# Turning the experts' rows in 32 by 32 blocks on VectorE, and loading them as 96 columns a partition group

## The chip, the cores and the metric

The kernel runs on one core of a Trainium2 chip. The engines are TensorE (PE), VectorE (DVE), ScalarE (ACT), GpSimd (POOL) and SyncE (SP, which here only issues DMAs). The metric is the device time of one execution in microseconds. The median of 3 runs of the kernel before is 709.5 us.

## The reference

A gated linear attention is followed by a mixture of experts; every token goes to two of eight experts.

```python
for t in range(S):                       # attention, 4 x 8 heads, 768 steps, 48 wide
    new_re = ar * S_re - ai * S_im
    new_im = ar * S_im + ai * S_re
    kv = np.einsum('bhd,bhe->bhde', k[:, :, t], v[:, :, t])
    S_re, S_im = (new_re + kv, new_im)
    y[:, :, t] = np.einsum('bhd,bhde->bhe', q[:, :, t], S_re)
...
# x: 3072 tokens of 384 floats, E = 8 experts, F = 1024
noisy_logits = x @ w_gate + np.log1p(np.exp(x @ w_noise)) * noise
top2 = np.argpartition(-noisy_logits, 2, axis=1)[:, :2]
...
for e in range(E):
    for k in range(2):
        mask = top2[:, k] == e
        h = np.maximum(x[mask] @ w1[e], 0.0)
        out[mask] += top2_w[mask, k, None] * (h @ w2[e])
```

## The kernel before

**The stage that the change leaves alone.** Up to about 280 us the kernel computes the attention in 24 tiles, finds each token's two experts and scatters its row (L497) into `xs` in DRAM: 400 floats, of which 0 to 383 are x, 384 to 391 the gates and 392 (`RNO`) the token's number, into the next free slot of the expert. Its order is written out by hand. Part of the work of experts 0 and 1 already lies in it.

**One expert.** An expert has 832 slots in two windows. Window 1 has 512 rows and lives in `xgb`, window 0 has 320 rows and lives in `xga`. `load_x` brings a window into SBUF with several whole rows on a partition (four of 1600 bytes side by side for window 1). The matmuls want x with its 384 columns on partitions, so `x_T` turns it: for each of the three blocks of 128 columns (kk = 0, 1, 2) PE multiplies tiles of 128 by 128 with an identity into PSUM (`px`, L625; 4 for window 1, 3 for window 0), ACT rounds the result to the high half of x (L630), DVE subtracts to get the low half (L631). It also copies the gates (`gw`, L615) and the token numbers (`ox`, L616) out of the rows.

`mm1` (L633 to L656) computes relu(x w1) in eight groups (f) of 9 matmuls, 3 for each kk: high by high, low by high, high by low. ACT does the relu (L651), DVE the low half (L655, tile `h`). `mm2_tile` (L691 on) computes one output tile of 128 rows: 24 matmuls into `po` (L698), an eviction by DVE that multiplies by the gate and adds to `ao` (L709), and a scatter by POOL into `out` (L710). Before that `gather_o` has fetched the old rows of `out` into `ao` (L674). Tiles 0, 1 and 2 belong to window 0, tiles 3 to 6 to window 1; tile 2 has 64 rows (L704, L707, L708). The weights come in pieces into `raw` (3 buffers) and are split by ACT (L586) and DVE (L587) into a high and a low half; `w1` is held twice (`e % 2`), `w2` once.

**What sets the order.** Outside the attention a scheduler arranges the instructions of each engine by their dependencies and the buffers; each engine then takes its queue strictly in order. `po` has 2 buffers, `ph` 4, `px` 2, `raw` 3; there is one `xgb` and one `xga`, so that the load of the next rows waits for the last reader of the present ones. `behind_of(a, name)` puts an instruction behind the latest of a kind on the same engine: `h` is the last relu on DVE, `m` the last matmul of mm1, `po` the last matmul of mm2.

**The order of the experts.** After mm2(0, 0) the program does mm1(1, 0), x_T(0, 1), mm1(0, 1), mm2(0, 1), x_T(1, 1), mm1(1, 1), mm2(1, 1), x_T(2, 1), mm2(1, 0), x_T(2, 0), where the pair is expert and window. Then comes a loop over experts 2 to 7, the tails of which the prediction speaks: mm1 of window 1; a conditional part `mm1_tail` (L658), which does mm1 of window 0 with 320 or with 256 rows and, in the first case, tile 2 too; then the tiles 3, 4, 5, 6, 0, 1, and after each of them one block of x_T of the next expert, in the order (1,0), (1,1), (1,2), (0,0), (0,1), (0,2) of window and kk. These transposes stand on PE behind the last matmul of the tile just done.

## Time and profile before

| | us |
|---|---|
| median of 3 runs | 709.5 |
| lowest and highest | 709.18, 710.33 |
| the profiled execution, its own time | 710.01 |
| its span, first to last instruction | 708.3 |
| lies outside the span | 1.7 |

The busy times of the engines are shares of the span and add up to more than one, since the engines run side by side. PE's matmuls are pipelined: a record lasts longer than the distance to the next one, so that distances of starts tell the pace. Idle time of an engine is put down to what ended it, in square brackets in a timeline; the chain of waits follows the end of the program back to its start.

### The profile page before, as it was taken

Reading aid. Unit: us, or ns where it says so; the run is one execution under the profiler, and the core shown is the slowest. Engines: PE = TensorE matmul, PEld = TensorE weight load, DVE = VectorE, ACT = ScalarE, POOL = GpSimd, SP = SyncE. Lnnn points to the kernel's source line nnn. Section 1 sums busy time; section 2 is a strip of 40 time slices with the busy share of each in tenths; the row PEclk is TensorE's granted clock in tenths of the full one; section 3 lists DMA queues with packets and bytes.
Section 4 is the critical chain, followed back from the end, with each engine's and each line's share of the span. In section 5 each row is a group of like instructions: output and inputs, shape, how many; then the busy total and the mean of one; then the engine's idle time right before and its main releaser. Section 6 shows DMA issues by size and latency. Waiting matters only on the chain.

```text
span 708.3 us, 13293 instructions
## 1 busy us (share of the span) xinstructions
PE 666.2 (94%) x5120; PEld 590.7 (83%) x5120; DVE 411.2 (58%) x919; ACT 328.0 (46%) x553; POOL 172.6 (24%) x183
## 2 busy tenths in 40 slices
PE   2599999999998999999999999999999999999995
PEld 0388887887776889898998998998999899899995
DVE  6799899999988747545237325425524524524311
ACT  7699888888775542324125215215313413413300
POOL 3000012451404225113224122322321411411311
PEclk9989999999999999999999999999999999999998
DMA  8877863654238516325128125425415515502201
GB/s 315 255 217 211 268 181 127 174 200 131 94 92 277 178 72 249 130 84 187 59 80 264 30 91 169 129 90 169 132 40 175 179 37 178 173 23 68 65 33 36
DMA packets 64190, 100.24 MB, mean 142 GB/s; under 512 B 26296, under 2 KB 46533, under 8 KB 64112
## 3 DMA queue, kind: packets, MB, share of 16 engines
q1 hardware_dynamic: 54752, 71.68, 32.7%
q0 software_dynamic: 9360, 27.54, 11.0%
q8 instruction: 46, 0.75, 0.4%
q14 instruction: 32, 0.26, 0.1%
HBM read 68.55 MB, written 31.69 MB: 142 GB/s over the span
## 4 chain that ended last, share of the span: by engine, by line
PE 80%; DVE 8%; ACT 5%; DMA 4%; issue 1%; SPq 1%; another core or an unknown queue 0%; POOL 0%; POOLq 0%; DVEq 0%; ACTq 0%
PE po L698 28%; PE ph L649 27%; PE ptr L354 4%; PE psc L363 4%; PE pY L412 2%; PE cum L307 2%; DMA raw<-in_moe_w_dram 2%; PE pY L414 2%; PE px L625 2%; PE pG L374 2%; PE po L704 2%; PE cum L331 1%; PE psc L649 1%; ACT t L248 1%; PE cum L427 1%
## 5 line engine op out<-in xcount | busy, mean ns | idle before, releaser
L698 PE MATMUL po<-w2h,h 128*128 128x384 f32 x768 | 203.9, 338 | 2.1 <-DVE ao L709 2.1
L649 PE MATMUL ph<-x,w1h 128*128 128x512 f32 (+2 forms) x720 | 187.2, 348 | 0.6 <-ACT x L630 0.5
L698 PEld LDWEIGHTS po<-w2h,h 128*128 128x128 f32 x768 | 139.4, 188 | 3.7 <-DVE ao L709 3.6
L649 PEld LDWEIGHTS ph<-x,w1h 128*128 128x128 f32 x720 | 125.7, 189 | 18.3 <-DVE h L655 1.3
L698 PE MATMUL po<-w2l,h 128*128 128x384 f32 x384 | 128.5, 335 | 0.0
L649 PE MATMUL ph<-x,w1l 128*128 128x512 f32 (+2 forms) x360 | 124.4, 347 | 0.0
L710 POOL DMA_INDIRECT out_dram<-ao,ox x52 | 50.9, 978 | 261.2 <-DVE ao L709 247.2
L497 POOL DMA_INDIRECT xs<-xr,sl x48 | 60.8, 1266 | 202.4 <-DVE qk L336 92.0
L655 DVE SCALAR_TENSOR_TENSOR h<-ph,h 128x512 fp32r<-128x512 f32 (+2 forms) x144 | 69.6, 505 | 67.5 <-ACT h L651 51.0
L651 ACT ACTIVATE h<-ph 128x512 fp32r<-128x512 f32 (+2 forms) x120 | 59.9, 507 | 102.0 <-PE ph L649 73.3
L709 DVE SCALAR_TENSOR_TENSOR ao<-po,gw,ao 128x384 f32<-128x384 f32 (+1 forms) x52 | 31.8, 614 | 125.1 <-PE po L698 124.8
L630 ACT CAST x<-px 128x512 fp32r<-128x512 f32 (+1 forms) x42 | 21.3, 518 | 125.5 <-PE px L625 125.5
L649 PEld LDWEIGHTS ph<-x,w1l 128*128 128x128 f32 x360 | 67.9, 189 | 7.9
L698 PEld LDWEIGHTS po<-w2l,h 128*128 128x128 f32 x384 | 72.2, 188 | 0.1
L674 POOL DMA_INDIRECT ao<-out_dram,ox x49 | 54.7, 1117 | 53.7 <-issue 31.7
L363 PE MATMUL psc<-qT,kT 112*128 112x128 f32 x384 | 54.1, 283 | 1.1 <-DVE h L655 0.6
L363 PEld LDWEIGHTS psc<-qT,kT 112*128 112x128 f32 x384 | 48.9, 196 | 5.9 <-issue 1.9
L586 ACT CAST w2h<-raw 128x768 fp32r<-128x768 f32 x32 | 26.5, 835 | 33.6 <-PE po L698 17.3
L414 PE MATMUL pY<-am,v 128*48 128x128 f32 x384 | 38.3, 275 | 1.6 <-DVE am L364 1.6
L587 DVE TENSOR_TENSOR w2l<-raw,w2h 128x768 fp32r<-128x768 f32 x32 | 30.4, 957 | 15.1 <-ACT w2h L586 14.2
L364 DVE TENSOR_TENSOR am<-psc,mask 128x512 f32<-128x512 f32 x48 | 32.8, 684 | 10.2 <-PE psc L363 8.6
L412 PE MATMUL pY<-qT,z 112*48 112x128 f32 x320 | 34.2, 279 | 0.2 <-DVE z L397 0.2
(211 smaller groups left out, 936.6 us busy)
## 6 DMA issues: line engine op xcount, KB each, us to landing
raw<-in_moe_w_dram SPq DMA_DIRECT2D x24, 512.0 KB
raw<-in_moe_w_dram SPq DMA_DIRECT2D x32, 384.0 KB
qk<-in_qk_dram SPq DMA_DIRECT2D x24, 384.0 KB
xgb<-xs SPq DMA_DIRECT2D x8, 800.0 KB
v<-in_v_dram SPq DMA_DIRECT2D x24, 192.0 KB
out_dram<-zero SPq DMA_DIRECT2D x12, 384.0 KB
re<-in_a_dram SPq DMA_DIRECT2D x11, 384.0 KB
im<-in_a_dram SPq DMA_DIRECT2D x11, 384.0 KB
```

The source lines that it names most:

```text
L363: key(f"P5{'ab'[half]}.{n}", nc.tensor.matmul(p[:, j, :], KT[n][:, h, :], QT[n][:, h, :], start=True, stop=True))
L364: LAST['am'] = nc.vector.tensor_mul(AM[n][:, 4 * half:4 * half + 4, :], p, mask[:, None, :].to_broadcast([128, 4, 128]))
L412: x = nc.tensor.matmul(o, Z[b][:, h, :], QT[n][:, h, :], start=True, stop=False, skip_group_check=True)
L414: x = nc.tensor.matmul(o, V[n][:, h, :], AM[n][:, h, :], start=not g, stop=True, skip_group_check=True)
L497: d = nc.gpsimd.indirect_dma_start(out=xs, out_offset=bass.IndirectOffsetOnAxis(ap=sl[:, kk, b:b + 1], axis=0), in_=XR[g][:, lo + b, :], i ...
L649: LAST['m'] = nc.tensor.matmul(p[:, :c], W1[e, kk][i][:, f * 128:(f + 1) * 128], XW[w, kk][:, j, 0:c], start=(m == 0), stop=(m == len(ms) ...
L651: nc.scalar.activation(h[:, 0:c], p[:, :c], AF.Relu)
L655: LAST['h'] = nc.vector.scalar_tensor_tensor(h[:, dst:dst + b - a], p[:, a:b], 0.0, h[:, a:b].bitcast(F32), op0=OP.max, op1=OP.subtract)
L674: nc.gpsimd.indirect_dma_start(out=ao[j][0:w, :], out_offset=None, in_=out, in_offset=bass.IndirectOffsetOnAxis(ap=OX[e][0:w, j:j + 1], ax ...
L698: LAST['po'] = key(f"PO.{e}.{j}", nc.tensor.matmul(p[:, :DM], HT[w, f][i][:, o:o + 128], W2[f // 2][k2][:, f % 2, :], start=(m == 0), stop ...
L709: nc.vector.scalar_tensor_tensor(a, p[0:n, :DM], g, a, op0=OP.mult, op1=OP.add)
L710: d = nc.gpsimd.indirect_dma_start(out=out, out_offset=bass.IndirectOffsetOnAxis(ap=OX[e][0:n, j:j + 1], axis=0), in_=a, in_offset=None, b ...
```

## The change

`load_x` brings window 1 of every expert, and window 0 of experts 2 to 7, in another layout. Four DMAs each fill one group of 32 partitions: group a gets columns 96a to 96a + 95, and partition p of it the rows p, p + 32, p + 64 and so on, as runs of 96 floats. A 32 by 32 block transposed in place then has column 96a + 3i + kk on partition 32a + i, if every third column is taken, so three DVE transposes (L656) give the three blocks of 128 columns. The order of x's columns over partitions and kk is another one than before, and `load_w1` takes the rows of w1 in that same order. ACT and DVE read the turned block from an SBUF tile `xt` (2 buffers) instead of `px`.

Gates and token numbers no longer lie on the partitions of their rows. They come as a tile `ex` (2 buffers) by one or two DMAs of 16 floats a row; the evictions read the gate from it (L739), `ox` is cast from it (L639 to L643). For experts 2 to 7 window 1 now holds the slots 0 to 511 and window 0 the slots 512 to 831. Window 0 of experts 0 and 1 is loaded as before and turned by PE, with every third column. The memset of `xgb` goes; x_T(0, 1) stands behind `h` on DVE instead of behind `m` on PE, and the transposes of the loop are no longer tied to a tile.

```diff
     def load_x(e, w, dst):
-        if w == 0:
-            t = CAP - 64 if e in TAILS else 256
+        if w == 0 and e not in TAILS:
             ds = [nc.sync.dma_start(dst[:, 0:2], x3[e, 0:256].rearrange("(p j) r -> p j r", j=2)),
-                  nc.sync.dma_start(dst[0:64, 2], x3[e, t:t + 64])]
+                  nc.sync.dma_start(dst[0:64, 2], x3[e, 256:320])]
...
-            o = 256 if e in TAILS else 320
-            nc.sync.dma_start(dst, x3[e, o:o + 512].rearrange("(p j) r -> p j r", j=4))
+            n = WIN[w][1]
+            x = blocks(dst, n)
+            o = CAP - n if w == 0 or e not in TAILS else 0
+            for a in range(4):
+                nc.sync.dma_start(x[32 * a:32 * a + 32], x3[e, o:o + n, 96 * a:96 * a + 96].rearrange("(t p) r -> p t r", p=32))
+            if w == 0:
+                return
+            EX[e] = ex = mt([128, 7, 16], F32, name="ex", bufs=2)
+            m = 6 if e in TAILS else 4
+            nc.sync.dma_start(ex[:, 0:m], x3[e, o:o + 128 * m, DM:ROW].rearrange("(m p) r -> p m r", p=128))
+            if e in TAILS:
+                nc.sync.dma_start(ex[0:64, 6], x3[e, CAP - 64:CAP, DM:ROW])
+
+    def blocks(t, n):
+        return t.rearrange("p j r -> p (j r)")[:, 0:3 * n].rearrange("p (t r) -> p t r", r=96)
...
-            nc.sync.dma_start(r, w1[e, kk * 128:(kk + 1) * 128, :])
+            nc.sync.dma_start(r, w1[e].rearrange("(p k) f -> k p f", k=KD)[kk])
...
         for kk in kks:
             x = XW[w, kk] = mt([128, 2, n], F32R, name=f"x{w}{kk}")
-            p = ps_tile("px")
-            for j in js:
-                o = 128 * (j - js[0])
-                gz = nc.tensor.transpose(p[:, o:o + 128], src_t[:, j - js[0], kk * 128:(kk + 1) * 128], ident)
+            if rows:
+                p = ps_tile("px")
+                for j in js:
+                    o = 128 * (j - js[0])
+                    c = src_t[:, j - js[0], 0:DM].rearrange("p (i k) -> p k i", k=KD)[:, kk]
+                    nc.tensor.transpose(p[:, o:o + 128], c, ident)
+            else:
+                p = mt([128, 512], F32, name="xt", bufs=2)
+                gz = nc.vector.transpose(p[:, :n].rearrange("p (t i) -> p t i", i=32), blocks(src_t, n).rearrange("p t (i k) -> p k t i", k=KD)[:, kk])
                 if (e, w) == (0, 1):
-                    behind_of(gz, 'm')
-                if last:
-                    behind_of(gz, last)
+                    behind_of(gz, "h")
...
-        a, g = ao[j][0:n, :], GW[e][0:n, j:j + 1]
+        a = ao[j][0:n, :]
+        g = GW[e][0:n, j:j + 1] if e not in TAILS and j < 3 else EX[e][0:n, extra(e, j), e:e + 1]
...
-    nc.vector.memset(xgb, 0.0)
...
-                x_T(e + 1, x[0], (x[1],), "po")
+                x_T(e + 1, x[0], (x[1],))
```

How the order moves, at three places. In the names a number behind the underline tells one use of a buffer; the two digits in `x10`, `h07` or `w1l21` are window and kk, window and f, and kk and e % 2.

PE at x_T(0, 1), right after mm1(1, 0), before:

```order
L649 MATMUL ph_3875<-x02_3488,w1l21_3530 128x320
L625 MATMUL px_3891<-ident_58,xgb_3684 128x128 x4
L625 MATMUL px_3899<-ident_58,xgb_3684 128x128 x4
L649 MATMUL ph_3917<-x10_3890,w1h00_2720 128x512
L649 MATMUL ph_3930<-x10_3890,w1h00_2720 128x512
L649 MATMUL ph_3943<-x10_3890,w1h00_2720 128x512
L625 MATMUL px_3907<-ident_58,xgb_3684 128x128 x4
L649 MATMUL ph_3917<-x10_3890,w1h00_2720 128x512
L649 MATMUL ph_3917<-x10_3890,w1l00_2721 128x512
```

PE at the same place, after:

```order
L678 MATMUL ph_3879<-x02_3488,w1l21_3530 128x320
L907 MATMUL px_4194<-flg_4189,ones_f_99 1x2
L678 MATMUL ph_3913<-x10_3893,w1h00_2720 128x512 x2
L678 MATMUL ph_3913<-x10_3893,w1l00_2721 128x512
L678 MATMUL ph_3913<-x11_3898,w1h10_2726 128x512 x2
L678 MATMUL ph_3913<-x11_3898,w1l10_2727 128x512
L678 MATMUL ph_3913<-x12_3903,w1h20_2732 128x512 x2
L678 MATMUL ph_3913<-x12_3903,w1l20_2733 128x512
```

The transposes are gone, a matmul of a flag (L878 before, L907 after) has moved up, and the first matmuls of three groups that stood between the transposes have gone back to their groups.

DVE at x_T(0, 1), before:

```order
L655 SCALAR_TENSOR_TENSOR h07_3874<-ph_3875,h07_3874 128x64
L615 COPY gw_2848<-xgb_3684 128x4
L616 CAST ox_2849<-xgb_3684 128x4
L631 TENSOR_TENSOR x10_3890<-px_3891,x10_3890 128x512
L631 TENSOR_TENSOR x11_3898<-px_3899,x11_3898 128x512
L631 TENSOR_TENSOR x12_3906<-px_3907,x12_3906 128x512
```

DVE at the same place, after:

```order
L684 SCALAR_TENSOR_TENSOR h07_3878<-ph_3879,h07_3878 128x64
L656 STREAM_TRANSPOSE xt_3894<-xgb_3684 128x512
L643 CAST ox_2848<-ex_3696 128x4
L656 STREAM_TRANSPOSE xt_3899<-xgb_3684 128x512
L660 TENSOR_TENSOR x10_3893<-xt_3894,x10_3893 128x512
L660 TENSOR_TENSOR x11_3898<-xt_3899,x11_3898 128x512
L656 STREAM_TRANSPOSE xt_3904<-xgb_3684 128x512
L660 TENSOR_TENSOR x12_3903<-xt_3904,x12_3903 128x512
```

Three transposes now stand between the last relu and the last subtraction, the third of them behind two subtractions, since `xt` has two buffers.

DVE in the tail of expert 2, from the end of the conditional part (the branch) to the second eviction, before:

```order
L663 UNCONDITIONAL_BRANCH
L709 SCALAR_TENSOR_TENSOR ao3_3680<-po_5015,gw_4473,ao3_3680 128x384
L631 TENSOR_TENSOR x10_5048<-px_5049,x10_5048 128x512
L709 SCALAR_TENSOR_TENSOR ao4_3681<-po_5056,gw_4473,ao4_3681 128x384
L631 TENSOR_TENSOR x11_5085<-px_5086,x11_5085 128x512
```

DVE at the same place, after:

```order
L692 UNCONDITIONAL_BRANCH
L660 TENSOR_TENSOR x12_5104<-xt_5105,x12_5104 128x512
L604 TENSOR_TENSOR w1l11_4994<-raw_4991,w1h11_4993 128x1024
L656 STREAM_TRANSPOSE xt_5139<-xga_94 128x320
L604 TENSOR_TENSOR w1l21_5000<-raw_4997,w1h21_4999 128x1024
L656 STREAM_TRANSPOSE xt_5173<-xga_94 128x320
L739 SCALAR_TENSOR_TENSOR ao3_3680<-po_5003,ex_4351,ao3_3680 128x384
L660 TENSOR_TENSOR x00_5138<-xt_5139,x00_5138 128x320
L660 TENSOR_TENSOR x01_5172<-xt_5173,x01_5172 128x320
L656 STREAM_TRANSPOSE xt_5207<-xga_94 128x320
L660 TENSOR_TENSOR x02_5206<-xt_5207,x02_5206 128x320
L739 SCALAR_TENSOR_TENSOR ao4_3681<-po_5041,ex_4351,ao4_3681 128x384
```

The turning of expert 3's x and two of the splits of its w1 have moved ahead of the eviction of tile 3, the first two blocks of it even ahead of the conditional part.

## Rows read from the trace of the kernel before

**Rows 1.** The page, parts 1 and 4: busy us, share, instructions; the chain by engine.

```profile
PE 666.2 (94%) x5120; PEld 590.7 (83%) x5120; DVE 411.2 (58%) x919; ACT 328.0 (46%) x553; POOL 172.6 (24%) x183
...
PE 80%; DVE 8%; ACT 5%; DMA 4%; issue 1%; SPq 1%; another core or an unknown queue 0%; POOL 0%; POOLq 0%; DVEq 0%; ACTq 0%
```

**Rows 2.** Groups by line and shape: busy us, mean ns | idle before, releaser.

```profile
L709 DVE SCALAR_TENSOR_TENSOR ao<-po,gw,ao 128x384 f32<-128x384 f32 x48 | 29.4, 614 | 124.8 <-PE po L698 124.8
L587 DVE TENSOR_TENSOR w1l<-raw,w1h 128x1024 fp32r<-128x1024 f32 x24 | 28.8, 1219 | 1.3 <-issue 0.9 <-ACT w1h L586 0.2
L631 DVE TENSOR_TENSOR x<-px,x 128x512 fp32r<-128x512 f32 x24 | 16.3, 689 | 8.5 <-ACT x L630 8.5
L625 PE MATMUL px<-ident,xgb 128*128 128x128 f32 x96 | 13.9, 273 | 0.0
L631 DVE TENSOR_TENSOR x<-px,x 128x320 fp32r<-128x320 f32 x18 | 8.8, 486 | 1.7 <-ACT x L630 1.7
L187 DVE MEMSET pY<- 128x512 f32 x1 | 0.5, 485 | 0.1
```

**Rows 3.** The chain in order of time: start us, us, what, instructions.

```profile
291.49 16.13 PE ph L649 x69
...
327.14 15.81 PE ph L649 x68
...
413.01 4.17 PE po L698 x24
417.62 4.17 PE po L698 x24
422.12 4.17 PE po L698 x24
```

**Rows 4.** PE's timeline after tile 3 of experts 2 and 7: start us, us.

```profile
407.26 0.60 PE L625 MATMUL px<-ident,xgb 128*128 128x128 f32 x4
408.14 0.45 PE L698 MATMUL po<-w2h,h 128*128 128x384 f32 x1 [0.27 <-DVE ao L709]
...
677.84 0.34 PE L698 MATMUL po<-w2h,h 128*128 128x384 f32 x1
678.88 0.44 PE L698 MATMUL po<-w2h,h 128*128 128x384 f32 x1 [0.71 <-DVE ao L709]
```

**Rows 5.** PE's timeline where x of experts 0, 1 and 2 is turned.

```profile
288.81 1.03 PE L625 MATMUL px<-ident,xgb 128*128 128x128 f32 x8
...
324.11 1.03 PE L625 MATMUL px<-ident,xgb 128*128 128x128 f32 x8
...
359.45 1.03 PE L625 MATMUL px<-ident,xgb 128*128 128x128 f32 x8
360.24 0.42 PE L698 MATMUL po<-w2h,h 128*128 128x384 f32 x1
...
372.01 0.82 PE L625 MATMUL px<-ident,xga 128*128 128x128 f32 x6
372.58 0.71 PE L649 MATMUL ph<-x,w1h 128*128 128x512 f32 x2
```

**Rows 6.** DVE's timeline at x_T(0, 1) and in the tail of expert 2.

```profile
289.48 0.56 DVE L655 SCALAR_TENSOR_TENSOR h<-ph,h 128x256 fp32r<-128x256 f32 x2 [0.70 <-ACT h L651]
...
404.58 0.61 DVE L709 SCALAR_TENSOR_TENSOR ao<-po,gw,ao 64x384 f32<-64x384 f32 x1
407.46 0.62 DVE L709 SCALAR_TENSOR_TENSOR ao<-po,gw,ao 128x384 f32<-128x384 f32 x1 [2.28 <-PE po L698]
```

**Rows 7.** SP's timeline, the DMA issue ahead of the load of expert 0's window 1.

```profile
281.10 0.33 SPq L542 DMA_DIRECT2D xga<-xs  x1
```

**Rows 8.** The page, part 3: packets, MB, share of 16 engines' span.

```profile
q1 hardware_dynamic: 54752, 71.68, 32.7%
```

**Rows 9.** Two stretches: length, busy us of PE, PEld, DVE, ACT, POOL, PEclk, DMA share, GB/s.

```profile
282.00:288.00 6.00, 6.00 (x41) 6.00 (x40) 4.66 (x20) 2.45 (x7) 0.99 (x1) 1.00 0.80 254
417.60:422.00 4.40, 4.40 (x29) 4.37 (x28) 1.10 (x3) 0.58 (x1) 0.97 (x1) 1.00 0.67 229
```

More of the change, by code (lines that the diff above doesn't have):

```diff
@@ L549, in load_x, with extra @@
         else:
-            o = 256 if e in TAILS else 320
-            nc.sync.dma_start(dst, x3[e, o:o + 512].rearrange("(p j) r -> p j r", j=4))
+            n = WIN[w][1]
[12 more added lines that the diff above has]
+        return t.rearrange("p j r -> p (j r)")[:, 0:3 * n].rearrange("p (t r) -> p t r", r=96)
+    def extra(e, j):
+        return (4, 5, 6, 0, 1, 2, 3)[j] if e in TAILS else j - 3
     mctx = ctx.enter_context(ExitStack())
@@ L561, in open_pool @@
         mpools.append(mctx.enter_context(tc.tile_pool(name=f"mp{len(mpools)}", bufs=1, reuse_waits="tile")))
-    W1, W2, XW, HT, GW, OX, DONE = {}, {}, {}, {}, {}, {}, {}
+    W1, W2, XW, HT, GW, OX, EX, DONE = {}, {}, {}, {}, {}, {}, {}, {}
     where = {}
@@ L605, in load_w2, with x_T @@
             split(rv, *W2[f2])
-    def x_T(e, w, kks=range(KD), last=None):
+    def x_T(e, w, kks=range(KD)):
         n = WIN[w][1]
@@ L610, in x_T @@
         js = JS[w]
-        if e not in GW:
-            GW[e] = mt([128, 7], F32, name="gw", bufs=2)
+        rows = w == 0 and e not in TAILS
+        if e not in OX:
             OX[e] = mt([128, 7], U32, name="ox", bufs=2)
         if 0 in kks:
-            gx = nc.vector.tensor_copy(GW[e][:, js[0]:js[-1] + 1], src_t[:, :, DM + e])
-            gy = nc.vector.tensor_copy(OX[e][:, js[0]:js[-1] + 1], src_t[:, :, RNO])
-            if (e, w) == (0, 1):
-                behind_of(gx, 'h')
-                behind_of(gy, 'h')
+            if rows:
+                GW[e] = mt([128, 3], F32, name="gw", bufs=2)
+                nc.vector.tensor_copy(GW[e], src_t[:, :, DM + e])
+                nc.vector.tensor_copy(OX[e][:, 0:3], src_t[:, :, RNO])
+            elif w == 1:
+                ex = EX[e][:, :, RNO - DM]
+                if e in TAILS:
+                    nc.vector.tensor_copy(OX[e][:, 3:7], ex[:, 0:4])
+                    nc.vector.tensor_copy(OX[e][:, 0:2], ex[:, 4:6])
+                    nc.vector.tensor_copy(OX[e][0:64, 2:3], ex[0:64, 6:7])
+                else:
+                    gy = nc.vector.tensor_copy(OX[e][:, 3:7], ex[:, 0:4])
+                    if e == 0:
+                        behind_of(gy, "h")
         for kk in kks:
             x = XW[w, kk] = mt([128, 2, n], F32R, name=f"x{w}{kk}")
-            p = ps_tile("px")
-            for j in js:
-                o = 128 * (j - js[0])
-                gz = nc.tensor.transpose(p[:, o:o + 128], src_t[:, j - js[0], kk * 128:(kk + 1) * 128], ident)
+            if rows:
+                p = ps_tile("px")
[3 more added lines that the diff above has]
+                    nc.tensor.transpose(p[:, o:o + 128], c, ident)
+            else:
+                p = mt([128, 512], F32, name="xt", bufs=2)
+                gz = nc.vector.transpose(p[:, :n].rearrange("p (t i) -> p t i", i=32), blocks(src_t, n).rearrange("p t (i k) -> p k t i", k=KD)[:, kk])
                 if (e, w) == (0, 1):
-                    behind_of(gz, 'm')
-                if last:
-                    behind_of(gz, last)
+                    behind_of(gz, "h")
             nc.scalar.copy(x[:, 0, :], p[:, :n])
```

## The prediction, made before the changed kernel had run

> **What bounds the kernel now.** I read the profile in four steps. First the page's busy shares and its chain of waits: TensorE (PE) is busy for 94% of the span and carries 80% of the chain, VectorE (DVE) is at 58% and carries 8% [rows 1]. So what PE no longer has to do comes off the time, unless PE then waits for whoever took the work. Second the groups of instructions, for the price of one operation on each engine [rows 2]. A record of a transpose says 273 ns, but matmuls are pipelined, so that figure must not be multiplied: the price of a transpose is what it pushes the next matmul back by. That is why, third, I read the chain and PE's timeline around each place where a block of x is turned [rows 3 to 5]. Fourth DVE's timeline, the queue of SP and the DMA shares, for what the moved work meets there [rows 6 to 9].
>
> The change takes 150 PE transposes out (96 of the 512-row windows, 54 of the 320-row windows of experts 2 to 7); 18 stay. In their place DVE runs 24 block transposes of 128x512 and 18 of 128x320. They stand at five kinds of places, which I cost one by one.
>
> **Part 1, the tails of experts 2 to 6 (five of them).** Before, after each output tile of 24 matmuls PE turned one block of the next expert's x: 4 transposes after tiles 3, 4, 5 and 3 after tiles 6, 0, 1. In the chain, a tile that begins at 413.01 lasts 4.17, so it ends at 417.18, and the next begins at 417.62: 0.44 for four transposes. From 417.62 + 4.17 = 421.79 to 422.12 it is 0.33 for three [rows 3]. The gap after tile 3 is different: from the transposes' start at 407.26 to the next tile at 408.14 it is 0.88, but the row says that the tile waited for DVE's eviction L709. Expert 7 has no transposes, and its gap is the same: the last matmul starts at 677.84 and takes a slot of 0.17, the next tile starts at 678.88, so 0.87 [rows 4]. So that gap stays, and the gain per expert is 2 x 0.44 + 3 x 0.33 = 1.87; five times that is **9.3 us**.
>
> **Part 2, a late eviction at expert 2.** The scheduler now puts DVE work between the end of the conditional tail and the eviction of tile 3: a subtraction of 128x512, two weight splits (w1l) and two block transposes of 128x320. Queued behind them is that eviction, and PE waits for it. DVE left the tail at 404.58 + 0.61 = 405.19 [rows 6]. To this come 0.69 + 2 x 1.22 [rows 2] and two transposes at 0.42 (below), 3.97 together: the eviction would start at 409.16 instead of 407.46, so **1.7 us** are lost. Experts 3 to 6 have only the subtraction and one transpose there, 1.1 us, which end before the tile does: nothing lost.
>
> **The price of a DVE transpose** is shown by no row. From below, the memset of 128x512, which reads nothing, took 485 ns; from above among full-rate work, the subtraction of 128x512 with two sources, one in PSUM, took 689 ns [rows 2]. With one source and one result in SBUF it should lie between them: I take 0.6, and 0.42 for 320 columns. Nothing rules out that a turn of 32 by 32 blocks with a source stride of 12 bytes runs at a fraction of that rate; this is the third rival.
>
> The Trainium skill, VectorE: DVE Perf Modes, section "The three transpose paths", gives 311 ns for a 128x128 bf16 transpose on VectorE, against 390 ns on TensorE. By that figure a 128x512 would be an estimated 1.24 us, and the time, with the sum below, about 705. The PE figure does not agree with the trace, where one more transpose costs PE 0.11 [rows 3], so that I do not build on the other figure either.
>
> **Part 3, x of expert 2.** Its two windows were turned during the last tiles of expert 1: eight transposes pushed PE from 359.45 to 360.24, 0.79 [rows 5], four more cost 0.44; the 320-row window cost 0.57 (372.01 to 372.58) [rows 5] and 0.33. Now DVE turns them during the four tiles of 4.17 each before that, beside evictions of 0.61; 3 x (0.6 + 0.69) + 3 x (0.42 + 0.49) = 6.6 us of work fit into 16.7. (0.49 and 0.69 are the subtractions of today [rows 2].) The gain is **2.1 us**.
>
> **Part 4, x of expert 1, window 1.** From the first transpose at 324.11 to the long run of matmuls at 327.14 there are 3.03 us, in which 4 of the 72 matmuls ran, at 15.81 / 68 = 0.2325 each [rows 3, 5]. So 2.1 us is the cost of the turn. About 0.2 of it, two small matmuls of a flag, remain elsewhere. DVE now turns the blocks between the evictions of the four tiles ahead; the last subtraction still stands behind the eviction of the last tile and may be up to 0.9 late. With 0.5 for that the gain is **1.4 us**.
>
> **Part 5, x of expert 0, window 1: a loss.** Here nothing can be turned early: on DVE the transposes are held behind the last relu (h) of the stage before, which ends at 289.48 + 0.56 = 290.04 [rows 6]. PE had started to turn at 288.81, and while it waited it ran three matmuls of other groups, which the new order no longer does. Step by step: transpose 290.64, cast of the tokens 290.71, transpose 291.31, ACT's first cast by then done, subtraction 291.95, subtraction 292.59, transpose 293.19, ACT's cast 293.78, subtraction 294.47. The eighth of the 72 matmuls needs that, so 65 remain from 294.47, at 16.13 / 69 = 0.2338 [rows 3]: they end at 309.67. Before, 69 matmuls from 291.49 ended at 307.62. So **2.05 us** are lost, between 1.7 and 2.3 with the two ends of the transpose's price.
>
> **Part 6, the loads.** The load of 512 rows becomes four DMAs of 512 runs of 384 bytes, with a small transfer of 64-byte runs beside. For a run of 384 bytes I have two bounds: by its bytes, 800 KB took 0.67 x 4.40 = 2.95 us of all 16 engines [rows 9], which is 22 ns on one engine; by the mean packet of the queue, 32.7% x 16 x 708.3 / 54752 = 68 ns, at 1309 bytes each [rows 8]. So 2048 runs take 2.8 to 8.7 us, and the 512 small ones up to 2.2. Only the load for part 5 has a deadline. It now goes first on the queue, from 281.10, where the other window stood [rows 7]; it lands between about 285 and 293.5, and DVE wants it at 290.04. I take 35 ns, nearer to the bytes, since the mean packet is three times as large: 4.5 us, landed in time, cost nothing. Every later load may start once DVE has turned the block before it. At expert 2 three of the four DMAs stand on SP's queue behind weights whose buffers come free only after the late splits of part 2, about three tiles (12.5 us) ahead of the next transpose; elsewhere the conditional tail's work lies between as well. Both bounds fit. Should that cover go, DVE's transposes wait, and behind them the evictions. The weights' rows are taken in another order with the same bytes. The memset that goes lies on DVE beside PE work: nothing.
>
> **Sum.** 9.3 - 1.7 + 2.1 + 1.4 - 2.05 = 9.05 us. The profiled execution took 710.0 and its span 708.3; the median is 709.5. So 701.0 for a run like the profiled one, and **700.4** against the median.
>
> The Trainium skill, DMA: Bandwidth & Descriptors, Specifications, wants at least 512 bytes in a transfer's run, and its Rules say of two transfers to disjoint partition halves "Don't bother". By these the four-way load of 384-byte runs is slower than the one it replaces. The first rival below works out from rows what that would do.
>
> **The rivals.**
> *The x load of part 5 comes late.* For it: the runs are short and scatters had just filled the engines, whose share was 0.80 at 254 GB/s while the load ran before [rows 9]. Against it: the load now goes first. At 68 ns and with the small runs DVE gets it at 293.5, 3.5 us late: 704. At 100 ns, 12.8 us plus 2.2, it is 6 us late: 706.5.
> *The gain is given back.* PE's gaps stay because an eviction or a weight split comes late in every tail, as at expert 2. If each of the five tails lost 1.7, that is 6.8 more: 707.2; with a load that is late too, about 709. Against it: in a tile of 4.17 DVE has an eviction, a transpose and a subtraction, 1.9 us [rows 2, 3].
> *Slower: the DVE transpose runs at a fraction of the assumed rate.* Let it take x more than 0.6. Part 5 loses 3x, part 4 up to 3x, part 2 about 1.3x (two shorter ones), and the tiles ahead of part 3, where four transposes stand before one eviction, about 1x once their slack is used: 8.3x. The gain of 9.05 is gone at x = 1.1, that is at 1.7 us for 128x512. At 2.2 us the loss is 13.3: 713.7. For it: no row shows the operation. Against it: no DVE row on 512 f32 columns is above 0.69 [rows 2].
>
> **Chances.** The forecast, 698 to 703.5: 0.58. Better, because the late eviction at expert 2 or the loss of part 5 stays out: 0.07. The late load, 703.5 to 707: 0.17. Given back: 0.09, most of it within 0.2% of 709.5 (708.1 to 710.9), which is about what a measurement of this kernel can tell from no change. Slower: 0.09. That makes faster 0.83, same 0.08, slower 0.09. The range leaves out the last two cases and little else: 696.5 to 707.
>
> **What would show it.** In the profile of the changed kernel: the tiles of each tail follow without the gaps of 0.33 and 0.44, while the one after tile 3 stays (part 1) and is some 2.6 at expert 2 (part 2); a row of the DVE transpose near 0.6 (0.5 to 0.7); PE idle for about 4 us around 290 to 294 behind DVE's subtraction (part 5), and by DMA instead if the load is late; PE busy less by about 150 x 0.11. The prediction is wrong if the transpose takes over 1 us, if PE waits for evictions in most tails, or if DMA ends waits that it did not end before.

## The result, and the profile after

The changed kernel takes 701.6 us at the median (4 runs, 700.7 to 702.2), the kernel before 709.4 in the same comparison. The ratio is 0.9887, with a 95% interval of 0.987 to 0.9904: faster by 7.8 us, 1.1%. The forecast was 700.4, in a range of 696.5 to 707.0. The profiled execution took 701.72, its span is 700.0 (before 708.3), so the profiles differ by 8.3.

The page after, parts 1, 3 and 4 (busy us, share, instructions; packets, MB, share of 16 engines; the chain by engine):

```profile
PE 651.8 (93%) x4970; PEld 577.9 (83%) x4970; DVE 435.8 (62%) x952; ACT 328.8 (47%) x553; POOL 176.8 (25%) x183
...
q1 hardware_dynamic: 83456, 71.69, 37.1%
...
PE 82%; DVE 8%; ACT 5%; DMA 2%; issue 1%; SPq 0%; POOL 0%; POOLq 0%; DVEq 0%; ACTq 0%
```

Against [rows 1], 14.4 us of work are gone from PE, which has 150 matmuls less, and 24.6 came to DVE. The shares of the chain are nearly the same: PE sets the end as before. The queue moves the same bytes in one and a half times as many packets [rows 8].

The groups that the change brought (busy us, mean ns):

```profile
L656 DVE STREAM_TRANSPOSE xt<-xgb 128x512 f32<-128x512 f32 x24 | 20.2, 857 | 0.0
L656 DVE STREAM_TRANSPOSE xt<-xga 128x320 f32<-128x320 f32 x18 | 10.8, 602 | 0.1
```

A transpose of 128x512 takes 0.86 us, not the 0.6 that the forecast took from [rows 2]. It is longer than the subtraction of the same size that reads two operands (0.69), which the forecast had held for the upper end.

The tails, first in the chain of the kernel before (start us, us, what): tile 2 of expert 2, tile 4 of expert 3 and mm1 of expert 4.

```profile
400.47 2.79 PE po L704 x16
...
461.43 4.46 PE po L698 x24
...
484.47 27.30 PE ph L649 x144
```

In the chain of the changed kernel: the output tiles of expert 0's window 1, tile 2 of expert 2, then mm1 of expert 3, its tile 3, its other five tiles and mm1 of expert 4.

```profile
310.85 16.85 PE po L728 x96
...
399.61 2.81 PE po L734 x16
...
430.07 25.42 PE ph L678 x144
455.49 4.24 PE po L728 x24
460.43 21.26 PE po L728 x120
481.69 26.92 PE ph L678 x144
```

Where [rows 3] had a gap of 0.44 or 0.33 after each tile, five tiles now stand as one piece of 21.26. The gap after tile 3 is still there (455.49 + 4.24 = 459.73 to 460.43). But a tile takes 4.24 instead of 4.17 or 4.18, which nothing in the forecast had foreseen.

PE's timeline at x_T(0, 1) after (in brackets the idle time ahead and what ended it):

```profile
289.55 0.19 PE L907 MATMUL px<-flg,ones_f 128*1 128x2 f32 x2
292.14 0.50 PE L678 MATMUL ph<-x,w1h 128*128 128x512 f32 x1 [2.40 <-ACT x L659]
...
295.12 0.51 PE L678 MATMUL ph<-x,w1h 128*128 128x512 f32 x1 [0.69 <-ACT x L659]
295.84 0.50 PE L678 MATMUL ph<-x,w1h 128*128 128x512 f32 x1 [0.22 <-DVE x L660]
```

And DVE's at the same place:

```profile
290.13 0.56 DVE L684 SCALAR_TENSOR_TENSOR h<-ph,h 128x256 fp32r<-128x256 f32 x2 [0.20 <-issue]
290.60 0.84 DVE L656 STREAM_TRANSPOSE xt<-xgb 128x512 f32<-128x512 f32 x1
...
291.40 0.86 DVE L656 STREAM_TRANSPOSE xt<-xgb 128x512 f32<-128x512 f32 x1
292.18 1.46 DVE L660 TENSOR_TENSOR x<-xt,x 128x512 fp32r<-128x512 f32 x2
293.55 0.86 DVE L656 STREAM_TRANSPOSE xt<-xgb 128x512 f32<-128x512 f32 x1
295.10 0.69 DVE L660 TENSOR_TENSOR x<-xt,x 128x512 fp32r<-128x512 f32 x1 [0.69 <-ACT x L659]
```

The order is the one that the forecast walked through. DVE's first transpose follows the last relu without a wait for DMA, so the load was there in time. PE stands still until the casts and subtractions come, and the eighth matmul starts at 295.84.

The tail of expert 2, PE's timeline at the end of tile 3 and the start of tile 4:

```profile
406.29 0.34 PE L728 MATMUL po<-w2h,h 128*128 128x384 f32 x1
408.77 0.45 PE L728 MATMUL po<-w2h,h 128*128 128x384 f32 x1 [2.15 <-DVE ao L739]
```

From 406.29 plus a slot of 0.17 to 408.77 it is 2.3 us, where [rows 4] had 0.88. Tile 4 waits for DVE's eviction of tile 3, which on DVE stands behind what the change moved ahead of it (the first and the last of its rows):

```profile
404.26 0.68 DVE L660 TENSOR_TENSOR x<-xt,x 128x512 fp32r<-128x512 f32 x1
...
408.15 0.57 DVE L739 SCALAR_TENSOR_TENSOR ao<-po,ex,ao 128x384 f32<-128x384 f32 x1
```

### The profile page after: what moved, and what is told of

The parts are those of the page before. It is cut to its first block, busy times and chain, and to the rows that moved or that the text cites. A ratio compares the mean times of both kernels' runs of the same rounds, so it can differ in the third digit from the quotient of the medians.

```text
span 700.0 us, 13088 instructions
## 1 busy us (share of the span) xinstructions
PE 651.8 (93%) x4970; PEld 577.9 (83%) x4970; DVE 435.8 (62%) x952; ACT 328.8 (47%) x553; POOL 176.8 (25%) x183
## 4 chain that ended last, share of the span: by engine, by line
PE 82%; DVE 8%; ACT 5%; DMA 2%; issue 1%; SPq 0%; POOL 0%; POOLq 0%; DVEq 0%; ACTq 0%
PE po L728 28%; PE ph L678 28%; PE psc L363 5%; PE ptr L354 4%; PE pY L412 2%; PE pY L414 2%; PE cum L307 2%; PE psc L678 2%; ACT t L248 2%; PE pG L374 2%; PE po L734 2%; PE cum L427 1%; PE cum L331 1%; DVE qk L336 1%; PE cum L436 1%
## 5 line engine op out<-in xcount | busy, mean ns | idle before, releaser
L728 PE MATMUL po<-w2h,h 128*128 128x384 f32 x768 | 199.8, 338 | 5.7 <-DVE ao L739 5.7
L740 POOL DMA_INDIRECT out_dram<-ao,ox x52 | 53.5, 1029 | 261.1 <-DVE ao L739 226.1
L739 DVE SCALAR_TENSOR_TENSOR ao<-po,ex,ao 128x384 f32<-128x384 f32 (+1 forms) x46 | 28.3, 615 | 101.8 <-PE po L728 101.5
L703 POOL DMA_INDIRECT ao<-out_dram,ox x49 | 56.3, 1148 | 44.4 <-issue 24.2
L659 ACT CAST x<-xt 128x512 fp32r<-128x512 f32 (+1 forms) x42 | 23.0, 551 | 49.1 <-DVE xt L656 46.0
```

What stands on the lines that cost most here:

```text
L703: nc.gpsimd.indirect_dma_start(out=ao[j][0:w, :], out_offset=None, in_=out, in_offset=bass.IndirectOffsetOnAxis(ap=OX[e][0:w, j:j + 1], ax ...
L728: LAST['po'] = key(f"PO.{e}.{j}", nc.tensor.matmul(p[:, :DM], HT[w, f][i][:, o:o + 128], W2[f // 2][k2][:, f % 2, :], start=(m == 0), stop ...
L740: d = nc.gpsimd.indirect_dma_start(out=out, out_offset=bass.IndirectOffsetOnAxis(ap=OX[e][0:n, j:j + 1], axis=0), in_=a, in_offset=None, b ...
```

## The experiments

The comparisons ran on several chips, on which the kernel before took 703.7 to 709.8 us. So each run is compared by its ratio to the kernel before on the same chip, and stages by rows of the profiles. The part of the kernel ahead of 267 us is edited by none of the experiments made from the changed kernel; even so it ended between 265.4 and 268.6 us in the profiles on chips where the kernel before took 709, and at about 260 in e12 and e13. Stages are therefore counted from there.

**x of expert 0 as before.** `e1_rows_first` undoes the change at the one place that the forecast called a loss: whole rows, PE's transposes behind mm1, gates and token numbers out of the rows.

```diff
+            if e == 0:
+                nc.sync.dma_start(dst, x3[0, 320:832].rearrange("(p j) r -> p j r", j=4))
+                return
             n = WIN[w][1]
...
-        rows = w == 0 and e not in TAILS
+        rows = w == 0 and e not in TAILS or (e, w) == (0, 1)
...
```

> Only x of expert 0, window 1, goes back to one load of whole rows and PE transposes; all else is the changed kernel. My theory: that place is the one that loses, because DVE's transposes are held behind the last relu there. In the changed kernel PE stands from 289.65 to 292.14 and again at 294.4 and 295.4, and the stage from the end of mm1(1, 0) to the first output matmul takes 21.3 us, against 18.8 before. So 2.5 us come back: about 699.1 against 701.6. Rival: the stage is long because the loads of that place are short runs which lie beside the scatters; then the time also falls, but DVE's rows in the changed kernel would show a DMA as what ended the wait, and they show none. Rival: the 0.7 us by which the stage already begins later come from the new loads too; then 3.2 us come back: 698.4.

Measured: 693.4 us, ratio 0.978 (0.9762 to 0.9798). That is 8 us less than the changed kernel, three times what was expected. The chain of e1, at x_T(0, 1) and in the tail of expert 3:

```profile
287.29 0.93 PE px L660 x8
...
306.03 16.66 PE po L737 x96
...
423.58 25.00 PE ph L687 x144
448.58 4.18 PE po L737 x24
453.46 21.09 PE po L737 x120
```

The place itself gave what was expected: 287.29 to 306.03 is 18.7, in the changed kernel from the flag's matmul at 289.55 to 310.85 it is 21.3, so 2.5 us. But further down, where nothing was edited, a tile takes 4.18 instead of 4.24, the five tiles 21.09 instead of 21.26, and mm1 of expert 3 25.00 instead of 25.42. Counted from the outputs at 267.7 and 265.4 to the end of the last tile, e1 has 5.9 us less: 2.5 at this place, 1.0 at expert 2 (see e3 below) and most of the rest by the pace. The other 2.3 lie ahead of that, where nothing was edited; their cause is not known, and they are not put down to the edit.

**The eviction first.** `e2_evict_first` moves two weight splits and the transposes of window 0 behind the eviction of tile 3 in the tail of expert 2, and with them the place where expert 3's w1 is loaded; `e3_both` makes this edit and that of e1.

```diff
             mm2_tile(e, int(j > 2), j)
+            if (e, j) == (2, 3):
+                LAST['ev3'] = LAST['ev']
+                load_w1(3)
...
+                if (e, w) == (3, 0):
+                    behind_of(gz, "ev3")
...
+        if ev:
+            behind_of(d, "ev")
...
```

> In the tail of expert 2 alone, two weight splits and the block transposes of window 0 of expert 3 are put behind the eviction of tile 3 on DVE. My theory: they cost PE 1.3 us (from the start of tile 3 to the start of tile 4 6.35 us in the changed kernel, 5.04 before, 4.94 at expert 3), so the gap falls to about 4.95 and the time by 1.3 to 1.4 us: 700.2. Rival: the splits moved back make the weights of expert 3 late, the loads behind them on the queue of SP too, and PE waits later in the same expert: no change, 701.6.

> Both edits together. If the two losses are independent stretches of PE's path, they add: 2.5 + 1.3 = 3.8 us less than the changed kernel, 697.8. If one of them only moved a wait elsewhere, less: 699 to 700.

Measured: e2 699.1, ratio 0.9853 (0.9832 to 0.9874). e3 693.4, ratio 0.9781, the same as e1. In the chain of e2 the conditional part's tile 2 begins at 400.15 and tile 4 at 407.88:

```profile
400.15 2.80 PE po L738 x16
...
407.88 21.26 PE po L732 x120
```

That is 7.73; in the changed kernel it was 399.61 to 408.77, 9.16. So 1.4 us came back at this place, as expected. That e3 gains nothing measurable over e1 has a reason in the rows: in e1 the scheduler had put the weight splits elsewhere, tile 4 of expert 2 came 8.11 after tile 2 (394.40 to 402.51), in e3 7.67. Only 0.4 was left to gain.

**Addresses or the stall?** Why does PE run slower in the changed kernel? `e10_layout` and `e11_layout_rows` have the instructions of the changed kernel and of e1, in the same order on every engine. Only the place of tiles in SBUF differs, above all of `x` and `h` of window 1, which PE reads: a tile drawn ahead of them had moved them up. In the first, the tiles `ex` and `xt` come from a pool behind all others; in the second, `ex` is drawn early.

```diff
+    xp = mctx.enter_context(tc.tile_pool(name="xp", bufs=1, reuse_waits="tile"))
+    where["ex"] = xp
+    where["xt"] = xp
     load_x(0, 1, xgb)
```

> The changed kernel with the same instructions in the same order on every engine; only the tiles ex and xt are drawn from a pool of their own behind all others, so that x and h of window 1 lie at the addresses that they have in e1_rows_first (x10 at 153696 instead of 154592, h10 at 165984 instead of 170976). Theory: PE's slower pace in the changed kernel (24 output matmuls of window 1 in 4.24 us, 4.18 before and in e1; 144 matmuls of mm1 of experts 3, 5 and 7 in 25.42, 25.00 in e1) comes from where these tiles lie. Then the paces return to 4.18 and 25.00, those of experts 2, 4 and 6 get a little slower (27.3, 27.3, 25.3), and 2.6 us come back: 699.0. Rival: the pace fell because PE stands still for 2.4 us at x_T(0, 1), which e1 does not do; then nothing changes: 701.6.

> The counterpart: e1_rows_first with the same instructions in the same order, but ex is drawn early, so that x and h of window 1 lie 896 bytes further up (x10 at 154592, as in the changed kernel). Theory of addresses: the paces become 4.24 and 25.42 for odd experts, and about 2.6 us are lost: 696.0. Rival, the stall: nothing changes, since PE does not stand at x_T(0, 1) here: 693.4.

Measured: e10 700.0, ratio 0.9869 (0.9852 to 0.9885); e11 696.9, ratio 0.981 (0.9792 to 0.9828). The chain of e10, mm1 and tiles of expert 3, and mm1 of expert 6:

```profile
428.90 25.00 PE ph L678 x144
453.90 4.18 PE po L728 x24
...
586.88 25.28 PE ph L678 x144
```

The same of e11:

```profile
426.93 25.42 PE ph L689 x144
452.35 4.24 PE po L739 x24
...
586.09 24.98 PE ph L689 x144
```

The paces went with the addresses, in both directions and to the hundredth, and the wait of 2.4 us at x_T(0, 1), the stall, has no part in them: e10 has the stall and the fast pace, e11 no stall and the slow one. mm1 of odd experts and of even ones (their `w1` lies in two sets of buffers) trade places. From the outputs at 267 us to the last tile e10 has 2.1 us less than the changed kernel, e11 1.9 more than e1. The medians moved by 1.8 and 3.0 thousandths of the kernel before's time, 1.3 and 2.1 us, with intervals that overlap; it is the rows that show the pace. The kernel before has e10's paces (tiles 4.17 or 4.18, mm1 of expert 4 27.30, of expert 7 25.00).

**Which addresses?** `e12_layout_mid` is e3 with an unused tile of 448 bytes.

> e3_both with an unused tile of 448 bytes ahead of x and h of window 1: the same instructions in the same order, x10 at 154144 and h10 at 166432, halfway between the two layouts seen. In the runs so far a stage of matmuls was slow where the two operands' first addresses lay 128 apart modulo 1024 (w1 of even experts 224 with x10 at 96; w1 of odd experts 864 or w2 864 with x10 or h10 at 992), and fast where they lay 256 apart. Here the distances are 320 for all three. If that distance decides, odd experts keep 25.00 and tiles 4.18, and even experts fall from 27.29 to 26.92 and from 25.28 to 24.98: about 1.3 us less than e3_both, 692.1. If the two layouts seen are just two states that trade even for odd experts, some stage goes back to its slow pace: 693.4 or more.

Measured: 688.7 on a chip where the kernel before took 703.7; ratio 0.9786 (0.9773 to 0.98), the same as e3. The chain, experts 3 and 6:

```profile
417.87 25.43 PE ph L691 x144
443.29 4.18 PE po L741 x24
...
576.51 25.13 PE ph L691 x144
```

The tiles stay fast, the odd experts' mm1 is slow again and the even experts' lies between. So the distance that I had read from two layouts is not the rule, and the rule stays open. What is shown is that the pace of the same matmuls depends on where their operands lie, by 0.6 to 1.7%.

**How much of DVE's new work is hidden?** `e4_turn_twice` does every DVE transpose twice.

```diff
-                gz = nc.vector.transpose(p[:, :n].rearrange("p (t i) -> p t i", i=32), blocks(src_t, n).rearrange("p t (i k) -> p k t i", k=KD)[:, kk])
+                for _ in range(2):
+                    gz = nc.vector.transpose(p[:, :n].rearrange("p (t i) -> p t i", i=32), blocks(src_t, n).rearrange("p t (i k) -> p k t i", k=KD)[:, kk])
...
```

> The changed kernel with every DVE transpose done twice into the same tile. If DVE's transposes are hidden but for x_T(0, 1) and the tail of expert 2, as my sum has it, three more transposes of 0.8 us there cost 2.4, and in the tail of expert 2 two more of 0.55 and one more weight split ahead of the eviction some 2.3; with up to 1.5 at x_T(1, 1): 706 to 708. Rival: DVE is near its limit in other stages as well (33 more us of work on an engine that is 62% busy), evictions come late in every tail: over 712.

Measured: 711.8, ratio 1.0028 (1.0012 to 1.0043), 10 us more than the changed kernel; between the two expectations, right at the edge of the rival's. Its chain in the tails of experts 3 and 5:

```profile
468.50 22.80 PE po L729 x120
...
578.12 21.27 PE po L729 x120
```

The last tails are untouched (21.27). In those of experts 2 and 3 the five tiles take 22.80 instead of 21.26, and this is not DVE's work but PE's clock. PE had waited 4.70 us for the late eviction at expert 2, and behind that wait the granted clock fell to 0.50, which is 1.2 of 2.4 GHz (length, busy of PE, PEld, DVE, ACT, POOL, clock, DMA share, GB/s):

```profile
414.00:417.00 3.00, 3.00 (x11) 3.00 (x10) 1.82 (x4) 0.46 (x1) 0.68 (x1) 0.50 0.92 282
```

Once the clock is back at 1.00, the tiles run as before. The same happens at expert 3 after a wait of 2.61 (0.51 from 468.5 to 472), and not at expert 4 after one of 1.26. So the 10 us are 1.8 at x_T(0, 1), 5.0 of longer waits for the eviction of tile 3 in experts 2, 3 and 4 (one weight split more had also moved ahead of that of expert 2) and 3.1 that the lower clock took from the tiles behind two of these waits. Of about 30 us of added DVE work some 7 pushed PE back directly.

The forecast's statement that the transposes are hidden beyond two places holds at their real price, with little to spare at tile 3 of experts 3 and 4. The third rival's mechanism is real: doubled, the transposes cost the whole gain, at 2 x 0.86 us, close to the 1.7 us at which the forecast let the gain vanish. That the two come so close is luck, since 3.1 of the 10 us are the clock's, which the rival did not have.

**Shorter runs.** `e5_runs_192` cuts each x load in two.

```diff
             for a in range(4):
-                nc.sync.dma_start(x[32 * a:32 * a + 32], x3[e, o:o + n, 96 * a:96 * a + 96].rearrange("(t p) r -> p t r", p=32))
+                for c in (0, 48):
+                    nc.sync.dma_start(x[32 * a:32 * a + 32, :, c:c + 48], x3[e, o:o + n, 96 * a + c:96 * a + c + 48].rearrange("(t p) r -> p t r", p=32))
```

> The changed kernel with each x load cut in two of 48 columns: twice the DMAs, runs of 192 bytes instead of 384. In the changed kernel a window of 512 rows, loaded alone, took 5.4 us of all 16 engines, 42 ns a run. If a run costs that whatever its length, the load takes 10.8 us; the one of x_T(0, 1) then lands some 4 us late and all others stay hidden: 705 to 706. If bytes decide, it takes the same 5.4 us: 701.6. If later loads are not hidden either, more than 708.

Measured: 701.6, ratio 0.9876 (0.9854 to 0.9898): no difference. Six us of the changed kernel and seven of e5, around the load of expert 2's window 1 alone (length, busy of PE, PEld, DVE, ACT, POOL, clock, DMA share, GB/s):

```profile
354.00:360.00 6.00, 6.00 (x36) 6.00 (x36) 3.80 (x8) 1.28 (x3) 1.19 (x1) 1.00 0.90 165
```

```profile
355.00:362.00 7.00, 7.00 (x42) 7.00 (x41) 4.32 (x9) 1.80 (x4) 2.17 (x2) 1.00 0.77 143
```

0.90 x 6 and 0.77 x 7 are 5.4 us of all 16 engines both times: twice the runs at half the length cost the same, at most 42 ns for 384 bytes and 21 for 192 (at most, because other transfers share the window: 165 GB/s over 6 us are 1.0 MB, and x has 0.8). So between these two lengths the bytes decide, not the number of runs, and the forecast's estimate of 35 ns for 384 bytes was near. But the whole rows of before moved as much in 2.95 us [rows 9]; what makes the new form take nearly twice that, for runs of either length, was not tried by itself.

The profile of e5 shows what the stall at x_T(0, 1) can cost besides itself. PE waits there for 2.40 us as in the changed kernel, but then runs at half the clock:

```profile
294.00:300.00 6.00, 5.71 (x13) 4.21 (x14) 1.38 (x2) 0.83 (x2) 0.00 (x0) 0.50 0.89 136
```

From the flag's matmul to the first output tile it took 23.7 us (288.74 to 312.42) instead of the changed kernel's 21.3. The profiles of e2, e4, e8, e10 and e13, which have the stall too, also show 0.50 just behind it; in e2, e10 and e13 the same stretch took 21.6, 21.7 and 22.6. The one profile of the changed kernel shows 1.00 there, and so do those of e1, e3, e11 and e12, which do not have the stall. The other executions of the changed kernel have no trace; how often they lose this is not known.

**What a transpose on PE costs.** `e6_before_twice` is the kernel before with every PE transpose done twice.

```diff
-                gz = nc.tensor.transpose(p[:, o:o + 128], src_t[:, j - js[0], kk * 128:(kk + 1) * 128], ident)
+                for _ in range(2):
+                    gz = nc.tensor.transpose(p[:, o:o + 128], src_t[:, j - js[0], kk * 128:(kk + 1) * 128], ident)
...
```

> The kernel before with each of its 168 PE transposes done twice in a row into the same place. It prices the transposes from the other side. By my sum a transpose costs PE 0.11 us where it stands on PE's path, and nothing after tile 3 of a tail, where the eviction is later: in five tails 2 x 0.44 + 3 x 0.33 = 1.87 each, 9.3 us, 12 and 9 of expert 2 2.1, 12 and 12 of experts 0 and 1 2.6, and up to 2 for the 18 of the attention stage; the gap of 0.88 after tile 3 grows too once eight transposes take 0.88 themselves, by 0 to 0.2 each. Together 14 to 17: 723 to 727. If the transposes ran in the shadow of something else (the eviction, the weight loads), the time would stay near 710, and PE's removed work would not explain the gain.

Measured: 724.8 against 703.7, ratio 1.0296 (1.0279 to 1.0313), 21 us more. The chain in the tail of expert 3:

```profile
468.33 0.87 PE px L626 x8
469.21 4.28 PE po L699 x24
...
474.36 4.19 PE po L699 x24
...
479.42 4.18 PE po L699 x24
484.26 4.18 PE po L699 x24
```

Eight transposes push the next tile by 0.87 (469.21 + 4.28 = 473.49 to 474.36), six by 0.66 (479.42 + 4.18 = 483.60 to 484.26). After tile 3 the eight, at 468.33, now just fill the 0.87 in which PE had waited for the eviction. That is the forecast's price of 0.11 and its exception. The time rose by more than expected because other waits joined in: a wait for a scatter of 4.8 us after x_T(1, 1), and waits for weights.

**Columns side by side.** `e8_contiguous` lets the transposes of experts 2 to 7 take 32 neighbouring columns, and loads w1's rows to match; `e13_w1_four` is the same with another form of that load:

```diff
-                nc.sync.dma_start(r, w1[e].rearrange("(a k i) f -> k a i f", a=4, k=KD)[kk])
+                for a in range(4):
+                    nc.sync.dma_start(r[32 * a:32 * a + 32], w1[e, 96 * a + 32 * kk:96 * a + 32 * kk + 32])
```

The edit of e8:

```diff
+            if e in TAILS:
+                nc.sync.dma_start(r, w1[e].rearrange("(a k i) f -> k a i f", a=4, k=KD)[kk])
...
-                gz = nc.vector.transpose(p[:, :n].rearrange("p (t i) -> p t i", i=32), blocks(src_t, n).rearrange("p t (i k) -> p k t i", k=KD)[:, kk])
+                gz = nc.vector.transpose(p[:, :n].rearrange("p (t i) -> p t i", i=32), blocks(src_t, n).rearrange("p t (k i) -> p k t i" if e in TAILS else "p t (i k) -> p k t i", k=KD)[:, kk])
```

> For experts 2 to 7 each block transpose takes 32 columns that lie side by side instead of every third (and the rows of w1 are loaded in the order that fits); experts 0 and 1 keep every third column, so one trace shows both forms. If the stride of 12 bytes is what makes the transpose 0.86 us long instead of the 0.6 that I took, the rows of experts 2 to 7 fall to about 0.6 (0.42 for 320 columns). If it is the operation's own rate, they stay at 0.86 and 0.60. The time moves little either way, 0.3 us at expert 2 at most: 701.3 to 701.6.

> e8_contiguous again (32 columns side by side in the block transposes of experts 2 to 7), but each w1 piece comes by four DMAs of 32 rows into 32 partitions each, instead of by one DMA whose rows are four groups of 32. In e8 ACT waited 73 us for w1 and the time was 775. If the form of that one DMA made it slow, ACT hardly waits for w1 here, and the time is near the changed kernel's, 700 to 702: the shorter transposes (0.70 instead of 0.86) lie beside PE's work. If the order of the rows of w1 itself is slow, or transfers into 32 partitions are, the time stays above 740.

Measured: e8 775.3, ratio 1.0918; e13 695.3 on a chip where the kernel before took 703.8, ratio 0.987 (0.9833 to 0.9907), as the changed kernel. The groups of e8:

```profile
L603 ACT CAST w1h<-raw 128x1024 fp32r<-128x1024 f32 x24 | 24.9, 1044 | 73.3 <-DMA raw<-in_moe_w_dram 73.3
L659 DVE STREAM_TRANSPOSE xt<-xgb 128x512 f32<-128x512 f32 x24 | 17.3, 735 | 9.1 <-DMA xgb<-xs 9.1
L659 DVE STREAM_TRANSPOSE xt<-xga 128x320 f32<-128x320 f32 x18 | 8.9, 498 | 0.1
```

And of e13:

```profile
L603 ACT CAST w1h<-raw 128x1024 fp32r<-128x1024 f32 x24 | 24.1, 1044 | 0.1
```

The 24 transposes of 128x512 in e8 are 18 of the new form and 6 of the old one at 0.86, so the new ones take (24 x 735 - 6 x 857) / 18 = 0.69 us, and those of 320 columns 0.50 instead of 0.60. So the stride of 12 bytes costs 0.16 of the 0.86, and the rest is the operation's own. It buys no time that a median shows, since the transposes of those experts were hidden. The 74 us that e8 lost came from its w1 loads: one DMA whose source is written as four groups of 32 rows kept ACT waiting for 73 us; as four DMAs, the same rows into the same partitions make no wait for w1. Part of the 74 came by way of the clock: PE waited for these weights, and the granted clock was 0.51 from 463 to 477, for example. The Trainium skill, DMA: Bandwidth & Descriptors, "Rules for kernel authors", has a rule that fits: a transfer whose outermost dimension has fewer than 16 entries is confined to at most that many engines. The pair of runs agrees with it, though no row here shows which engines carried the load.

## Why the prediction was right, point by point

Its sum was 9.05 us; the profiles differ by 8.3, the medians by 7.8. The steps, each against the rows after:

| step | forecast | rows |
|---|---|---|
| tails of experts 2 to 6 | +9.3 | +8.75 |
| late eviction at expert 2 | -1.7 | -1.5 |
| x of expert 2 | +2.1 | +2.4 |
| x of expert 1 | +1.4 | +1.9 |
| x of expert 0 | -2.05 | -2.5 |
| pace of PE's matmuls | none | no row of its own, see below |
| ahead of 267 us | none | -0.6 |

The rows add up to 8.45, and the stages between these places come out even to within 0.2. That the sum is so near is in part luck: the forecast left out the pace, so that the tails came out 0.55 short, and it missed 0.45 at x of expert 0 and 0.6 ahead of 267 us; against this, x of experts 1 and 2 gained 0.8 more than it said and the late eviction cost 0.2 less. At expert 1 the 0.5 set aside for a late subtraction was not needed: PE waits nowhere there. For the 0.6 ahead of 267 us the cause was not looked for; there the granted clock between 30 and 60 us was 0.83 in this profile and 0.89 before.

**The tails.** Before, mm1 of expert 4 began 23.04 after tile 4 of expert 3 (461.43 to 484.47), after it is 21.26: 1.78. The five together, 1.69 + 1.78 + 1.79 + 1.76 + 1.73, are 8.75. The forecast's 1.87 is right for an unchanged pace: in e1, at 21.09, it is 1.95. The mechanism and the exception after tile 3 were right, as e6 shows from the other side.

**The eviction at expert 2.** From tile 2 to tile 4 it was 7.67 before (400.47 to 408.14) and 9.16 after. DVE's list took 3.89 from 404.26 to 408.15, where the forecast had 3.97; its transposes were longer than assumed, but each of these rows starts up to 0.1 before the one ahead of it ends. e2 gave the 1.4 back.

**The loss at x of expert 0.** Its mechanism was right, and its size missed mainly in the step that the forecast had marked as unknown: the transpose's price. From the last relu's end to the end of the last subtraction it took 5.10 (290.69 to 295.79) instead of the 4.43 of the forecast's walk. The three transposes are some 0.5 of this, since the next instruction starts about 0.8 after each (291.40 to 292.18, for example) instead of 0.6. The rest is small, among it that the walk counted 0.64 for a subtraction where [rows 2] has 0.69. The 65 matmuls behind it then ran in 15.00 instead of 15.20. e1 showed the place to be worth 2.5 us. What the forecast left out is the lower clock that can follow this stall (e5).

**The loads.** No DVE transpose of the changed kernel waited for a DMA. A run of 384 bytes cost at most 42 ns, between the forecast's bounds of 22 and 68. The first rival did not occur, and with e5's eight DMAs too DVE's first transpose at x_T(0, 1) stood directly behind the relu. The rival's landing times of 285 and 293.5 hold 1.1 to 1.5 us beyond the terms that the prediction names, and that for 100 ns does not; neither came into play.

**What was missing** is the pace. The forecast treated a matmul's price as a constant of the trace before. The change drew `ex` (896 bytes) and `xt` ahead of x and h of window 1, moved their addresses, and PE's matmuls lost 2.1 us, by e10; e10's own lead is shortened by 0.4 through the lower clock at x_T(0, 1). About half of the loss lies in the rows of the table. The other half is made up by gains outside them that the forecast did not have either: mm1 of experts 3, 5 and 6 had taken 0.2 to 0.4 us longer before than in e10, and the end after the last tile became 0.4 shorter.

`e1_rows_first` (693.4 where the kernel before took 709.2) beats both kernels by 2.2 and 1.1%, and e3 and e12 are equal to it within their intervals. Of its 8 us against the changed kernel the rows account for 5.9; with these alone the change would be worth about 1.9%.

**The third rival** had 9% and a threshold of 1.7 us for the transpose of 128x512. At 0.86 it stayed far from it, and below the estimate of 1.24 that the prediction set beside its 0.6 (with its own slope of 8.3 that estimate gives 705.7, not 705). e4, with 1.7, took 0.3% longer than the kernel before; 3.1 of its 10 us against the changed kernel are the clock's.

## What to carry to other kernels

On an engine that is busy 94% of the time, work is priced by how far it pushes the next instruction back, not by its record's length, and moving it to another engine pays only where that engine can do it early: look for the one place at which it cannot (here the first use, behind the last relu) and leave that one as it was. After a change that adds a tile, compare the pace of untouched loops before and after; if it moved, try the same instructions with the tile drawn from somewhere else. Where TensorE waits for about two microseconds or more, read the granted clock of the stretch behind the wait as well, since the wait can cost more than its own length. And when a load is given a new shape, look at the outermost dimension of the transfer: the same bytes, in two shapes, kept their reader waiting for 73 us or not at all.

## What the runs showed that I had not expected

The pace of the same matmuls depends on where their operands lie in SBUF: 24 output matmuls took 4.18 or 4.24 us, 144 of mm1 25.00, 25.42 or (even experts) 24.98, 25.13 and 25.28, each tied to one layout and the same to 0.03 us in the profiles with that layout, where the clock was at 1.00. A simple rule by the distance of the two operands fell with e12, and which addresses are good stays open.

Behind waits of PE of 1.9 to 4.7 us, at x_T(0, 1) and at late evictions, the granted clock often fell to 0.50, but not always: the changed kernel's own waits of 2.40 and 2.15 were not followed by it in its profile. Five tiles behind such a wait took 22.80 us instead of 21.26 (e4).

A DVE transpose of 32 by 32 blocks took 0.86 us for 128x512 floats with a source stride of 12 bytes and 0.69 with neighbouring ones, as much as a subtraction of that size.

A w1 load whose source is written as four groups of 32 rows kept its reader waiting for up to 8 us at a time; the same as four DMAs, not at all.
